# A feed-forward tail in a decode kernel: W_down loaded by 1 KB rows so that gate and up weights are read as contiguous columns

## The chip, the cores and the metric

The kernel runs on one core of one Trainium2 chip. Times are device microseconds (us) of that core, one number for each execution. A whole execution measures about 1.8 us longer than the span that its trace shows, so whole times are compared with whole times and spans with spans.

PE is the tensor engine's matmul side, PEld its weight loads (they overlap the matmuls), DVE the vector engine, ACT the scalar engine, SP the engine that issues the loads (its sequencer is SPq). PV is the product of the attention weights with V. A load has landed at the last of its semaphore updates in the trace; the views give the time from issue to landing to 0.1 us only.

## The reference, cut to what matters

One decode step for two sequences: layer norm, attention over a cache of 8192 positions and 32 heads, residual, layer norm, a gated feed-forward block, residual.

```python
B, D, F = 2, 512, 1376                    # one token each
h  = x + attention(layernorm(x), k_cache, v_cache, wq, wo)
d  = layernorm(h)
gate, up = d @ W_gate, d @ W_up           # [2, 1376]
hid = gate * (gate > 0) * up
out = h + hid @ W_down                    # [1376, 512]
```

The two caches are 268 MB; the three feed-forward matrices are 4.2 MB together.

## The kernel before

The caches stream through four buffers `slot[0..3]` of 4 MB. When the last K tile has left `slot[0]`, the three feed-forward matrices are loaded into it, with the last V tile between them, cut into four parts:

```python
for k, w in enumerate((B_W_up, B_W_gate)):
    nc.sync.dma_start(
        slot[0][:, k * DC * F:(k + 1) * DC * F],
        w.rearrange("(p c) n -> p (c n)", c=DC)).then_inc(sem_w, 16)
load_v(p + 1, vparts)                     # last V tile, four parts
nc.sync.dma_start(
    slot[0][:, 2 * DC * F:2 * DC * F + 10 * D],
    B_W_down[0:10 * 128].rearrange("(p r) n -> p (r n)", r=10)).then_inc(sem_wd, 16)
# rows 1280..1375 were loaded at the start, into wd_last [96, D]
```

Partition p holds ten successive rows of W_down, 10p to 10p + 9: one run of 10 KB. Tile f of the hidden layer therefore has to be the columns f, f + 10, f + 20, ... of W_up and W_gate, so that column 10p + f comes out on partition p:

```python
wup, wgt = ...                            # each [128, DC = 4, F = 1376] in slot[0]
def ffn_in(dst, w, f0, f1):
    for f in range(f0, f1):               # FC = 11 tiles: ten of 128 columns, one of FR = 96
        fw = 128 if f < 10 else FR
        for c in range(DC):
            i = nc.tensor.matmul(
                dst[0:fw, f * B:(f + 1) * B],
                lhsT=w[:, c, f:1280:10] if f < 10 else w[:, c, 1280:F],
                rhs=d_b[:, c * B:(c + 1) * B], start=(c == 0), stop=(c == DC - 1))
    return pe.run(i)

FH = 6
t_u = ffn_in(Sp[1], wup, 0, FC)                                    # PE S, 44 matmuls
t_g = (ffn_in(Op[1], wgt, 0, FH), ffn_in(Wp, wgt, FH, FC))         # PE O, 24; PE W, 20
# ... DVE: u_sb <- up; hd <- max(gate, 0) * u_sb, in two halves ...
pe.wait((sem_wd, 32))
# ... 44 matmuls with W_down as weights (line 515), then the last sum o_c and the output
```

The weights are the stationary operand (`lhsT`), and each matmul streams only two columns (B = 2): every matmul of this tail is a weight load of 128 x 128 with next to no arithmetic behind it.

The softmax here doesn't subtract the row's maximum and nothing guards it: scores larger than these inputs give would overflow.

## Time and profile before

| | before |
|---|---|
| whole time, median | 679.52 us (679.33 to 679.94, 4 runs) |
| span of the trace | 678.2 us |
| HBM read rate over the span | 414 GB/s |
| last wait for V is over, its PV matmuls start | 664.28 us |
| gate and up matmuls (line 473) on the chain | 2.79 + 1.39 + 1.25 = 5.43 us |
| W_down lands | 641.29 + 26.65 = 667.94 us |
| first matmul with W_down starts | 672.68 us |

From the page of the kernel before: the DMA share of 40 equal slices of the span in tenths (9 is 90% or more), what the DMA moved in GB/s, and what the chain that ended last is made of.

```profile
DMA  9999999999999999999999999999999999999991
GB/s 375 427 432 376 430 431 430 429 428 430 428 429 430 432 430 432 430 432 427 430 428 429 426 429 427 431 432 432 431 432 430 429 431 425 429 429 393 416 406 58
DMA 73%; DVE 24%; PE 1%; issue 1%; SPq 0%; DVEq 0%
```

The loads bound the kernel, in every slice but the last one. The only place where a faster matmul can count is that last slice, where no load is waited for any more. The chain of waits in order of time (start, duration, what) shows it, from the last V part on:

```profile
640.14 24.09 DMA slot<-in_A_v_cache_dram
...
664.28 1.45 PE O L334 x48
...
667.03 0.17 DVE d_b L458
667.21 0.14 issue
667.34 2.79 PE S L473 x44
670.13 1.39 PE O L473 x24
671.51 1.25 PE W L473 x20
672.77 0.05 PE S L502 x2
672.82 1.49 PE O L515 x44
```

After 664.28 us everything is a chain of PE and DVE pieces, and line 473 is more than half of it. Why it is slow stands in the groups of instructions by shape (line, engine, operation, out<-in, shapes, count; busy us, mean ns of one; idle before):

```profile
L334 PEld LDWEIGHTS O<-e,slot 128*128 128x128 bf16 x256 | 7.3, 105 | 1.7 <-DMA slot<-in_A_v_cache_dram 1.7
L473 PEld LDWEIGHTS S<-d_b,slot 128*128 128x128 bf16 x40 | 2.4, 156 | 0.4 <-issue 0.4
L515 PEld LDWEIGHTS O<-hd,slot 128*128 128x128 bf16 x40 | 1.4, 118 | 0.0
L473 PEld LDWEIGHTS S<-d_b,slot 128*96 128x96 bf16 x4 | 0.4, 194 | 0.0
```

Four weight loads, three of them of the same 128 x 128 size. Line 334 (PV) reads contiguous columns, line 515 columns 4 elements (8 bytes) apart, line 473 columns 10 elements (20 bytes) apart. Loads and matmuls overlap, so the durations are not the pace; the pace is the distance between the starts of two matmuls in the trace: 26.7, 33.3 and 58.3 ns in the same order. The tile of 96 columns, contiguous though it is, comes every 80 ns.

### The profile page before, as it was taken

How to read it: one execution, taken by the hardware profiler on the slowest of the kernel's cores; microseconds unless marked ns; L12 is line 12 of the kernel's file. 1: busy time of each engine (PE TensorE's matmuls, PEld its weight loads, DVE VectorE, ACT ScalarE, POOL GpSimd, SP SyncE). 2: the span in 40 equal slices, each digit the busy share in tenths (PEclk: the TensorE clock that was granted, in tenths of full speed). 3: DMA queues.
4: the chain of work that ended last, by engine and by line, in shares of the span. 5: the costliest groups of instructions: out<-in, count | busy, mean ns of one | idle time of the engine just before them, and what ended most of it. 6: DMA issues, size and time to landing. Idle time of an engine off the chain costs nothing.

```text
span 678.2 us, 14430 instructions
## 1 busy us (share of the span) xinstructions
PE 297.5 (44%) x6596; PEld 269.5 (40%) x6596; DVE 493.6 (73%) x428; ACT 202.3 (30%) x523; POOL 1.7 (0%) x11
## 2 busy tenths in 40 slices
PE   2552254344544424454443435444344634433356
PEld 2442244333434424343443334434334634433355
DVE  1774577778777768877777787776788867777981
ACT  0630332233333213333322333332223333222430
POOL 0000000000000000000000000000000000000000
PEclk9999999556556556556555565555565555555555
DMA  9999999999999999999999999999999999999991
GB/s 375 427 432 376 430 431 430 429 428 430 428 429 430 432 430 432 430 432 427 430 428 429 426 429 427 431 432 432 431 432 430 429 431 425 429 429 393 416 406 58
DMA packets 14785, 281.97 MB, mean 416 GB/s; under 512 B 1443, under 2 KB 5637, under 8 KB 5765
## 3 DMA queue, kind: packets, MB, share of 16 engines
q1 hardware_dynamic: 14720, 281.06, 97.4%
q8 instruction: 51, 0.84, 0.5%
q14 instruction: 10, 0.07, 0.0%
q10 hardware_dynamic: 4, 0.00, 0.0%
HBM read 281.05 MB, written 0.00 MB: 414 GB/s over the span
## 4 chain that ended last, share of the span: by engine, by line
DMA 73%; DVE 24%; PE 1%; issue 1%; SPq 0%; DVEq 0%
DMA slot<-in_A_k_cache_dram 69%; DVE prod L366 15%; DVE tb L374 5%; DMA slot<-in_A_v_cache_dram 4%; DVE prod L374 3%; DVE scores L381 1%; PE S L473 0%; PE O L515 0%; PE O L334 0%; PE O L473 0%; PE W L473 0%; SPq L353 0%; SPq L135 0%; SPq L428 0%; PE W L309 0%
## 5 line engine op out<-in xcount | busy, mean ns | idle before, releaser
L366 DVE TENSOR_TENSOR prod<-slot,q_b 128x6144 bf16<-128x6144 bf16 x64 | 214.9, 3358 | 132.3 <-DMA slot<-in_A_k_cache_dram 131.1
L334 PE MATMUL O<-e,slot 128*128 128x2 bf16 x4096 | 118.7, 165 | 239.7 <-ACT e L267 120.2
L334 PEld LDWEIGHTS O<-e,slot 128*128 128x128 bf16 x4096 | 114.5, 104 | 243.9 <-ACT e L267 122.8
L397 ACT ACTIVATE kT<-T 128x1024 bf16<-128x1024 bf16 x128 | 126.8, 1022 | 169.9 <-PE T L391 168.8
L391 PE MATMUL T<-ident,slot 128*128 128x128 bf16 x1024 | 123.4, 307 | 76.7 <-DMA slot<-in_A_k_cache_dram 75.2
L374 DVE TENSOR_TENSOR tb<-prod 128x3072 bf16<-128x3072 bf16 (+1 forms) x128 | 148.2, 1158 | 4.4
L391 PEld LDWEIGHTS T<-ident,slot 128*128 128x128 bf16 x1024 | 100.2, 141 | 79.7 <-DMA slot<-in_A_k_cache_dram 78.2
L267 ACT ACTIVATE e<-scores 64x48 bf16<-64x48 f32 x128 | 32.8, 256 | 253.6 <-DVE scores L381 252.0
L374 DVE TENSOR_TENSOR prod<-tb 128x1536 bf16<-128x1536 bf16 (+1 forms) x128 | 84.2, 658 | 4.4
L259 PE MATMUL S<-qT,kT 128*128 128x2 bf16 x1024 | 48.4, 168 | 38.6 <-ACT kT L397 37.3
L259 PEld LDWEIGHTS S<-qT,kT 128*128 128x128 bf16 x1024 | 41.0, 107 | 57.4 <-ACT kT L397 57.4
L381 DVE TENSOR_REDUCE scores<-prod 128x48 f32<-128x384 bf16 x64 | 35.4, 553 | 2.2
L267 ACT ACTIVATION_READ_ACCUMULATOR e<-scores 64x1 f32 x128 | 23.6, 185 | 0.0
L267 ACT ACTIVATE e<-S 64x32 bf16<-64x32 f32 x64 | 13.0, 203 | 15.1 <-PE S L259 14.3
L267 ACT ACTIVATION_READ_ACCUMULATOR e<-S 64x1 f32 x64 | 12.8, 201 | 0.7
L241 ACT ACTIVATE q_b<-O 128x512 bf16<-128x512 f32 x8 | 4.3, 596 | 15.5 <-PE O L236 15.5
L212 DVE CAST qT<-W 128x64 bf16<-128x64 f32 x1 | 0.2, 225 | 11.9 <-PE W L207 11.9
L309 PE MATMUL W<-O_sb,X 128*128 128x2 bf16 (+1 forms) x136 | 5.0, 172 | 7.0 <-DVE O_sb L297 7.0
L309 PEld LDWEIGHTS W<-O_sb,X 128*128 128x128 bf16 x136 | 4.8, 118 | 7.2 <-DVE O_sb L297 7.2
L207 PE MATMUL W<-xlT,X 128*128 128x2 bf16 x128 | 3.6, 165 | 8.5 <-DMA X<-in_A_wq_dram 8.5
L207 PEld LDWEIGHTS W<-xlT,X 128*128 128x128 bf16 x128 | 3.5, 104 | 8.6 <-DMA X<-in_A_wq_dram 8.6
L285 DVE TENSOR_REDUCE zr<-O 128x16 f32<-128x48 f32 (+1 forms) x4 | 0.8, 204 | 8.3 <-PE O L277 8.3
(58 smaller groups left out, 44.4 us busy)
## 6 DMA issues: line engine op xcount, KB each, us to landing
slot<-in_A_k_cache_dram SPq DMA_DIRECT2D x32, 4096.0 KB, 27.8
slot<-in_A_v_cache_dram SPq DMA_DIRECT2D x31, 4096.0 KB, 32.1
X<-in_A_wq_dram SPq DMA_DIRECT2D x1, 4096.0 KB, 12.2
X<-in_A_wo_dram SPq DMA_DIRECT2D x1, 4096.0 KB, 49.0
slot<-in_A_v_cache_dram SPq DMA_DIRECT2D x1, 1536.0 KB, 21.6
slot<-in_B_W_up_dram SPq DMA_DIRECT2D x1, 1376.0 KB, 9.8
slot<-in_B_W_gate_dram SPq DMA_DIRECT2D x1, 1376.0 KB, 16.3
slot<-in_A_v_cache_dram SPq DMA_DIRECT2D x1, 1280.0 KB, 24.1
```

Source lines behind the costliest of these rows:

```text
L207: i = nc.tensor.matmul(Wp[:, h * B:(h + 1) * B], lhsT=wq[:, c, h * Dh:(h + 1) * Dh], rhs=lT[:, c * B:(c + 1) * B], start=(c == 0), stop=(c ...
L241: t_cp[m] = act.run(nc.scalar.activation(out=q_b[:, m * 512:(m + 1) * 512], in_=Op[m % 2][:], func=ACT.Copy))
L259: i = nc.tensor.matmul(Sp[p % 2][:, 2 * jj:2 * jj + 2], lhsT=kT[n % 3][:, k * 128:(k + 1) * 128], rhs=qT[:, 2 * p:2 * p + 2], start=True, ...
L267: t = act.run(nc.scalar.activation(out=e_t[p % 2][q, j0:j0 + nj, a], in_=src(q, a), func=ACT.Exp, scale=inv_sqrt_dh, accum_out=zs[q, 2 * p ...
L285: dve.run(nc.vector.tensor_reduce(out=zr[:, 2 * p0:2 * p1], in_=zbank(k)[:, 64:64 + n * (NCH + 1)].rearrange("p (n k) -> p n k", k=NCH + 1 ...
L309: i = nc.tensor.matmul(Wp[:, c * B + b0:c * B + b1], lhsT=wo_m[:, h, c, :], rhs=Ov[:, h // 2, h % 2, b0:b1], start=first[0], stop=last, sk ...
L334: i = nc.tensor.matmul(Op[k % 2][:, col:col + 2], lhsT=v_t[:, j, :], rhs=e_t[p % 2][:, j, :], start=(nmm == 0), stop=(nmm == J - 1))
L366: t_dm = dve.run(nc.vector.tensor_tensor(out=prod[:], in0=k_t[:, c * JC:(c + 1) * JC, :], in1=qv, op=ALU.mult))
L374: dve.run(nc.vector.tensor_tensor(out=o, in0=cur[:, :, 0:half], in1=cur[:, :, half:w], op=ALU.add))
L381: t_s = dve.run(nc.vector.tensor_reduce(out=sc[:], in_=cur, axis=AX.X, op=ALU.add))
L391: i = nc.tensor.transpose(Tp[n % 3][:, k * 128:(k + 1) * 128], k_t[:, j, :], ident[:])
L397: t_ev[n] = act.run(nc.scalar.activation(out=kT[n % 3][:], in_=Tp[n % 3][:], func=ACT.Copy))
```

## The change

The intent is to read the gate and up weights in contiguous columns. Tile f becomes columns 128f to 128f + 127, so hidden unit 128r + p sits on partition p, and W_down has to follow: row 128r + p goes to partition p, place r. In HBM those rows are 128 KB apart, and the load becomes 1280 runs of 1 KB in place of 128 runs of 10 KB.

```diff
                         nc.sync.dma_start(
-                            slot[0][:, 2 * DC * F:2 * DC * F + 10 * D],
-                            B_W_down[0:10 * 128].rearrange("(p r) n -> p (r n)", r=10)).then_inc(sem_wd, 16)
+                            slot[0][:, 2 * DC * F:2 * DC * F + 10 * D].rearrange("p (r n) -> p r n", n=D),
+                            B_W_down[0:10 * 128].rearrange("(r p) n -> p r n", p=128)).then_inc(sem_wd, 16)
...
-                                dst[0:fw, f * B:(f + 1) * B], lhsT=w[:, c, f:1280:10] if f < 10 else w[:, c, 1280:F],
+                                dst[0:fw, f * B:(f + 1) * B], lhsT=w[:, c, f * 128:f * 128 + fw],
```

## The prediction

> **What bounds the kernel now.** The load of the caches: the page shows 414 GB/s over the 678.2 us span, DMA busy above 90% in 39 of 40 slices, and a chain that is 73% DMA. The change touches only the tail. In the chain in order of time the last V piece is waited for until 664.2 us; then PE and DVE run alone to the end. There the gate and up matmuls (L473) run from 667.34 to about 672.63 us, 5.3 us, all on the chain; the down matmuls (L515) follow until 674.3.
>
> **Removed.** Start to start in the trace, at a granted clock of 0.50: the 80 full-width L473 matmuls, whose weight columns step 10 elements (20 bytes), come every 58.3 ns; their weight loads last 155 ns. The 8 narrow ones (96 columns, contiguous already) come every 80 ns. Matmuls with contiguous weights of the same 128 x 128 shape come every 26.7 ns (L334, PV, at 0.50; L207 the same at 1.00), weight load 104 ns. With a step of 4 elements (L309, L515) it is 33.3 ns. So reading the weights sets the pace. The Trainium skill, page "SBUF — State Buffer", section "Specifications (TRN2)", says cachelines are 16 bytes and each crossing to a new line costs; the trace's 26.7 / 33.3 / 58.3 ns for steps of 2 / 8 / 20 bytes agree in order.
> Saving: 80 x (58.3 - 26.7) = 2.5 us, all on the critical path: DVE's copy of u (0.18 us) and the first hd product (0.17 us) keep hiding behind the remaining gate matmuls (0.64 and 0.75 us), and vh is ready by 668.0.
>
> **Added.** W_down's 1.31 MB come in 1280 rows of 1 KB instead of 128 of 10 KB. In the trace a 10 KB packet takes 385 ns (38.5 ns per KB); W_o, loaded in 1 KB rows with the same 128 KB pitch, moved at about 348 GB/s against 430, that is 47 ns per KB and engine. An engine has 80 KB of W_down, so the load takes 3.8 us rather than 3.1: 0.7 us later. Now it lands at 667.9 us (issue 641.29, 26.6 us to landing), 4.7 us before its first use at 672.7. After: estimated landing 668.7, first use about 670.15. About 1.4 us of slack is left, so the slower load stays hidden. It is queued behind V, so V's landing should not move. Its issue may block the queue longer (a K issue after W_o was held 24.6 us), which harms nothing: only the output follows.
>
> **Predicted.** 679.57 - 2.5, plus a little for the chance that W_down is waited for: 677.2 us, range 676.4 to 678.7. Faster by over 2%: 0.5%; within 2%: 99%; slower: 0.5%. The gain is about 0.35%, four times the spread of the three runs (0.6 us).
>
> **What would show it.** L473 every 27 ns (weight load 104 ns), its 88 matmuls in 2.8 us; L515 starting 2.9 us after the d_b subtraction ends and still every 33 ns; the V landing near 664.2; W_down's time to landing 27 to 28 us, and no DMA piece of W_down in the chain of waits; about 1150 more packets under 2 KB.
>
> **What would make it wrong.** W_down landing after 670.2, if its many rows are issued or moved slower than W_o's by the few late engines; then up to all of the gain goes into a wait before L515. Or its small packets on early engines slowing the V pieces that others still load. Or contiguous weights not at 26.7 ns here. A change of over 2% would need the cache stream itself to move, which nothing here touches.

## The result, and the profile after

| | before | after |
|---|---|---|
| whole time, median | 679.52 us (679.33 to 679.94, 4 runs) | 677.57 us (677.15 to 677.79, 4 runs) |
| span of the trace | 678.2 us | 675.6 us |
| last wait for V is over, its PV matmuls start | 664.28 us | 664.30 us |
| line 473 on the chain | 5.43 us | 2.92 us |
| W_down lands | 667.94 us | 641.34 + 26.93 = 668.27 us |
| first matmul with W_down starts | 672.68 us | 670.19 us |

The ratio is 0.997 (95% interval 0.9952 to 0.9987). Ratios here are the mean time of one kernel's fast runs over that of the other's of the same rounds, so not quite the ratio of the medians quoted. By the 2% rule the verdict is "same", and the gain is clear of the noise all the same.

The page of the kernel after, the same lines (slices, and the chain's shares):

```profile
DMA  9999999999999999999999999999999999999993
DMA 73%; DVE 24%; PE 1%; issue 1%; SPq 0%; DVEq 0%
```

Nothing moved in the stream of the caches. The chain of waits in order of time:

```profile
640.20 24.05 DMA slot<-in_A_v_cache_dram
...
664.30 1.46 PE O L334 x48
...
667.05 0.17 DVE d_b L458
667.23 0.14 issue
667.36 1.53 PE S L473 x44
668.89 0.64 PE O L473 x24
669.53 0.75 PE W L473 x20
670.28 0.05 PE S L502 x2
670.33 1.48 PE O L515 x44
```

The two chains run in step to 0.02 us up to line 473, and from there the new one is shorter by 5.43 - 2.92 = 2.51 us. No load stands between the gate matmuls and line 515: W_down is not waited for. The groups by shape, of the kernel after:

```profile
L473 PEld LDWEIGHTS S<-d_b,slot 128*128 128x128 bf16 x40 | 1.2, 104 | 0.4 <-issue 0.4
L515 PEld LDWEIGHTS O<-hd,slot 128*128 128x128 bf16 x40 | 1.4, 117 | 0.0
L473 PEld LDWEIGHTS S<-d_b,slot 128*96 128x96 bf16 x4 | 0.4, 186 | 0.0
```

The wide tiles of line 473 now load like those of line 334, and in the trace their matmuls start every 26.7 ns. Line 515, whose weights keep their layout, did not change. The narrow tile did not either: 80 ns from start to start, 8 times.

The clock that the throttle granted to PE differs between the two traces as a whole (0.607 and 0.551 on average), but not where it matters. Stretches of the span in the kernel before and then in the kernel after (columns: length; busy us of PE, PEld, DVE, ACT, POOL; granted clock; DMA share; GB/s):

```profile
667.30:670.30 3.00, 2.96 (x50) 2.99 (x51) 0.72 (x5) 0.00 (x0) 0.00 (x0) 0.50 0.02 5
```

```profile
667.30:670.30 3.00, 2.94 (x94) 2.97 (x95) 0.96 (x6) 0.00 (x0) 0.00 (x0) 0.50 0.04 11
```

At the same clock of 0.50, and PE busy throughout in both, the stretch that held 50 matmuls now holds 94: all 88 of line 473 and the first of the lines behind it.

### The profile page after: what moved, and what is told of

It reads as the page before. It is cut to its first block, busy times and chain, and to the rows that moved or that the text cites. A ratio compares the mean times of both kernels' runs of the same rounds, so it can differ in the third digit from the quotient of the medians.

```text
span 675.6 us, 14430 instructions
## 1 busy us (share of the span) xinstructions
PE 294.0 (44%) x6596; PEld 266.2 (39%) x6596; DVE 493.6 (73%) x428; ACT 202.0 (30%) x523; POOL 1.7 (0%) x11
## 2 busy tenths in 40 slices
DMA packets 15936, 281.97 MB, mean 417 GB/s; under 512 B 1442, under 2 KB 6916, under 8 KB 7044
## 4 chain that ended last, share of the span: by engine, by line
DMA 73%; DVE 24%; PE 1%; issue 1%; SPq 0%; DVEq 0%
DMA slot<-in_A_k_cache_dram 69%; DVE prod L366 15%; DVE tb L374 5%; DMA slot<-in_A_v_cache_dram 4%; DVE prod L374 3%; DVE scores L381 1%; PE S L473 0%; PE O L515 0%; PE O L334 0%; SPq L353 0%; SPq L135 0%; SPq L428 0%; PE W L473 0%; PE O L473 0%; PE W L309 0%
```

## The experiments

The comparison with the reference passed for every run below, those that are wrong included (two of them pair the wrong hidden units with the rows of W_down, two read arbitrary columns). So passing says nothing here about the order of rows and columns; that the changed kernel, and the one with a wider last tile below, pair them correctly is argued from the index arithmetic alone.

Theory A: the gain is the 80 wide weight loads of line 473, 58.3 to 26.7 ns each, all of it on the chain, and the load by 1 KB rows costs nothing because it hides in a slack. Rival B: the 1 KB rows give part of it back (four runs showed a mean gain of 2.06 us, the traces 2.5 us). Rival C: the load by rows itself brings part of the gain.

### The two halves apart, and more rounds

Three of the four kernels on one chip (the fourth, e4_wide_last, is further below). `e0_after` is the changed kernel. `e1_cols_only` has only the new columns:

```diff
-  lhsT=w[:, c, f:1280:10] if f < 10 else w[:, c, 1280:F],
+  lhsT=w[:, c, f * 128:f * 128 + fw],
```

`e2_load_only` is the changed kernel with the old line put back there, so only the load differs from before.

> The changed kernel again, with more rounds, because its four runs gave 2.0 us of gain (679.52 to 677.57) where the two traces' tails differ by 2.5 us (output issued 674.79 and 672.29). Theory A (the gain is 2.5 us and the rest is spread of the runs): mean gain 2.3 to 2.7 us. Theory B (something outside the tail gives 0.4 to 0.5 us back, for example V arriving later): gain 1.8 to 2.2 us, and the last V wait would end at 664.6 or later in the trace. Either way the profile should again show the last V wait ending near 664.25 and the output issued 8.0 us after it.

> Only the matmul half of the change: contiguous weight columns, W_down still loaded by 10 KB rows (the result is wrong on purpose). Theory A: the whole gain is here, the same as the full change, 2.3 to 2.7 us, with W_down landing near 667.9. Rival B (the 1 KB rows give part back): this one is faster than the full change by 0.4 to 0.5 us. Rival C (the load itself brings part of the gain): this one gains clearly less than the full change.

> Only the load half of the change: W_down by 1 KB rows, matmul columns still 10 elements apart (the result is wrong on purpose). Theory A: no change, within 0.2 us of the kernel before, W_down landing 0.3 to 0.7 us later than 667.9 with over 4 us to spare. Rival B: slower by 0.4 to 0.5 us. Rival C: faster.

The kernel before had 679.91 us (679.59 to 680.65, 9 runs). "Tail" is the distance, in the one trace of each kernel, from the start of the last 48 PV matmuls to the start of the last sum o_c; "W_down after V" is its landing counted from the same start.

| | whole time, median (5 runs each) | difference of the means | tail | W_down after V |
|---|---|---|---|---|
| before (its first trace) | 679.91 us | | 674.41 - 664.28 = 10.13 us | 3.66 us |
| e0_after | 677.30 us (676.95 to 677.51) | -2.63 us | 671.57 - 663.94 = 7.63 us | 3.98 us |
| e1_cols_only | 677.30 us (677.04 to 677.52) | -2.63 us | 671.25 - 663.63 = 7.62 us | 3.79 us |
| e2_load_only | 679.75 us (679.53 to 680.19) | -0.09 us | 674.09 - 663.95 = 10.14 us | 3.98 us |

The ratios to the kernel before are 0.9963, 0.9963 and 1.0 (intervals 0.995 to 0.9975 twice, and 0.9987 to 1.0014). These intervals reach about 0.9 us to each side, too far to rule out the 0.4 us of rival B. What rules it out is the comparison within the call: the means of e0_after and e1_cols_only agree to 0.01 us, with 0.5 to 0.6 us between the slowest and the fastest run of each, and their tails agree to 0.01 us. So the columns alone give the whole gain, and the load alone gives none and takes none: rivals B and C fall. The chain of waits has the new pace in e1_cols_only and the old one in the load-only kernel:

```profile
666.69 1.53 PE S L473 x44
668.22 0.64 PE O L473 x24
668.86 0.75 PE W L473 x20
```

```profile
667.02 2.79 PE S L473 x44
669.80 1.39 PE O L473 x24
671.19 1.25 PE W L473 x20
672.44 0.05 PE S L502 x2
672.50 1.48 PE O L515 x44
```

The expectation for e0_after of a V wait ending near 664.25 was missed by 0.3 us: it ended at 663.94; the output was issued 8.0 us after that, as expected. Over the twelve traces of these kernels it ends between 663.63 and 664.46, while the tail of a given kernel repeats to 0.02 us. So the spread from run to run lies outside the tail: ahead of it, and also behind it, where the time from the start of o_c to the end of the whole execution runs from 5.3 to 5.9 us in the same twelve traces. That is large enough for small sets of runs to give 2.06, 2.63 and (below) 2.22 us for the same change. What moves the V landing and the end was not traced.

### How much slack W_down has

A dummy load of 5 or 9 rows of 1 KB for each partition, into a buffer that nobody reads, is put between V and W_down (in the second kernel 9 in place of 5):

```diff
+        pad = sb("pad", [128, 5 * D], BF16)
...
                         load_v(p + 1, vparts)
+                        nc.sync.dma_start(
+                            pad[:], B_W_down[0:5 * 128].rearrange("(p r) n -> p (r n)", r=5)).then_inc(sem_pad, 16)
```

> The changed kernel with a dummy load of 5 KB rows (0.66 MB) between V and W_down, which puts W_down off by about 40 KB per engine x 38.5 ns = 1.5 us, to about 669.9. The changed kernel's first W_down matmul came at 670.33 and W_down landed at 668.3, so there should be 2.0 us to spare: no change of time within 0.3 us if that is the true slack. If the slack is smaller than I read it (if the wait for W_down already ends last), the time rises by up to 1.5 us.

> The same with 9 KB rows (1.18 MB): W_down put off by about 2.8 us to about 671.1, that is 0.8 us after it is wanted. If the slack is 2.0 us the time rises by 0.6 to 1.0 us over the changed kernel and W_down's load appears in the chain of waits before L515. If the matmuls did not really need to wait for it, no change.

Measured beside the kernel before at 679.95 us (679.75 to 680.11, 7 runs): with 5 KB 677.01 us (676.92 to 677.5, 4 runs), with 9 KB 678.18 us (677.9 to 678.51, 4 runs). The first keeps the whole gain (2.81 us by the means). In its trace W_down lands at 641.63 + 28.1 = 669.7 us, and its first matmul starts at 670.08, not held up; the tail is 671.81 - 664.18 = 7.63 us. The second gives part of the gain back: its tail is 672.93 - 664.46 = 8.47 us, 0.85 us longer than the 7.62 us of the changed kernel, within the expected 0.6 to 1.0. (By whole times it is 1.08 us slower than the 5 KB kernel; its V wait also ended 0.28 us later.) The start of the second's chain of waits, and one of its waits (who waited for whom: us, times, longest):

```profile
642.32 28.82 DMA slot<-in_B_W_down_dram
671.14 0.05 issue
671.19 1.64 PE O L519 x44
```

```profile
PE O L519 <- DMA slot<-in_B_W_down_dram: 0.7, 1, 0.7
```

Now the load is on the chain, and V, DVE and the gate matmuls are not: W_down lands at 671.14 us, and line 519 (line 515 of the kernel before) starts 0.05 us later. So the wait is real, and the changed kernel passes it with 670.19 - 668.27 = 1.92 us to spare. A version with much more to load in that place would pay for it.

### What the pace of a weight load depends on

The changed kernel, with another column step for each of the 20 wide tiles (a wrong result), so that one trace holds a ladder of steps:

```diff
-  lhsT=w[:, c, f * 128:f * 128 + fw],
+  lhsT=ladder(f, c, k),       # slot[0][:, c * F : c * F + step * 127 + 1 : step], step = STEPS[k][f]
```

> A measurement of the weight read by itself: the changed kernel with a different column step for every tile of L473 (wrong result on purpose): up tiles 0 to 9 with steps 1, 2, 3, 4, 5, 6, 7, 8, 9, 10 elements of 2 bytes, gate tiles 0 to 9 with steps 12, 14, 16, 20, 24, 32, 10, 8, 2, 1. Theory L (cost is per new 16-byte line): spacing rises from 26.7 ns at step 1 to about 58.3 ns at step 8, by the number of lines that 128 columns touch, and stays at 58.3 ns for every step from 8 to 32; step 4 is 33.3 ns. Rival S (cost grows with the step): step 16 and 32 come clearly slower than step 10. Rival F (a step of any size loses a fast mode): step 2 is already at 58 ns. If pairs of 8-byte units count, step 3 lies at or below step 4.

> The ladder again in another order (wrong result on purpose): up tiles 0 to 9 with steps 24, 10, 32, 16, 12, 20, 9, 7, 5, 3 elements, gate tiles 0 to 9 with steps 48, 40, 28, 24, 10, 18, 4, 6, 2, 1. In the first ladder the spacing followed the number of 16-byte lines up to step 8 (60 ns) and was 58 to 69 ns beyond it, with step 24 at 69 ns and step 10 once at 65 and once at 60 ns. If the level beyond 8 is flat and the rest is the place in the sequence, step 24 comes at 58 to 63 ns here in at least one of its two places. If step 24 has a cost of its own, both are near 69 ns. Steps 5, 7, 9, 6 should repeat 39, 54, 61 and 47 ns whatever their place.

Each ran once, in 678.64 and 679.39 us, which is of no use beyond the trace.

Each tile has four matmuls. The distance from the start of a matmul to that of the one behind it, without the first of the four, averaged over the other three (worked out from the starts in the two traces; granted clock 0.50):

```
step, elements            1     2     3     4     5     6     7     8     9    10
16-byte lines touched    16    32    48    64    80    96   112   128   128   128
first ladder, up, ns   27.7  26.7  28.3  31.7  38.7  47.3  53.7  60.7  62.0  62.7
second ladder, ns      26.7  26.7  27.7  31.7  39.0  47.3  54.7     -  59.0  62.3, 58.3

step, elements           12    14    16    18    20    24    28    32    40    48
first ladder, gate, ns 60.7  62.7  61.7     -  58.3  68.7     -  66.0     -     -
second ladder, ns      62.7     -  62.3  62.0  59.3  69.7, 68.0  61.3  67.3  61.7  66.3
```

Up to step 3 a floor of about 27 ns holds. From step 4 to 8 the pace rises in a straight line with the number of 16-byte lines that 128 columns touch: 31.7 ns for 64 lines, 47.3 for 96, 60.7 for 128, which is 0.47 to 0.50 ns a line. With 8-byte units step 4 would already be the worst, with 32-byte units step 16 would be twice step 8; neither is so. Beyond 8, where every column is on a line of its own, it stays between 58 and 70 ns. The expectation of a strictly flat 58.3 ns was too simple: step 24 came at 68 to 70 ns in all three of its places, and 32 and 48 at 66 to 67, while 20, 28 and 40 did not. (Step 10 came at 58 to 63 ns, with 59.0 in a second place of the first ladder.) For 24, in three places, that is a property of the step and not of its place in the sequence; 32 stood in two places and 48 in one only. What makes it stays open. In the second ladder steps 5, 6 and 7 repeated within 1 ns, as expected; step 9 came at 59.0 ns, where 61 was expected. Rival S (the cost grows with the step) and rival F (any step loses a fast mode) fall: step 48 costs no more than step 24, and step 2 costs nothing.

The durations of the loads vary too, as far as a view that mixes the steps can show it. The first ladder's loads of the up half, as the view of one line shows them (min, median and max of a load in ns, mixed steps and the narrow tile):

```profile
L480 PEld LDWEIGHTS S<-d_b,slot x44: 104/145/198, 666.9 to 668.8; 128*128 128x128 bf16 x40, 128*96 128x96 bf16 x4
```

The Trainium skill says in "SBUF — State Buffer", section "Specifications (TRN2)", that SBUF has 16-byte cachelines and needs at least two hits a line for full bandwidth. The ladder agrees with the line size and nearly with the threshold: step 4, two hits a line, costs 5 ns over the floor; step 5 costs 12.

### The tile of 96 columns

The narrow tile comes every 80 ns although its columns touch. The page "TensorE: Matmul & The Clock Gate" of the Trainium skill, section "Weight-path perf modes — Fast Weight Load (FWL) and DoubleRow", says the fast weight load needs the full 128 columns, and its section "LDWEIGHTS (loading the stationary operand)" puts a load at the number of columns over 1.2, in ns. An estimate from that page is 96 / 1.2 = 80 ns; the trace has 80 ns from start to start (the load itself is recorded with 186 to 194 ns). The section does not say for which mode its figure holds: for 128 columns it gives 107 ns, and the pace here is 26.7. If the missing fast mode is the reason, more columns should be cheaper. `e4_wide_last` computes columns 1248 to 1375, and the 32 that tile 9 has already meet rows of zeros:

```diff
-  wd_last = sb("wd_last", [FR, D], BF16)
+  wd_last = sb("wd_last", [128, D], BF16)
-  nc.sync.dma_start(wd_last[:], B_W_down[F - FR:])...
+  nc.sync.dma_start(wd_last[128 - FR:], B_W_down[F - FR:])...
+  pool.run(nc.gpsimd.memset(wd_last[0:128 - FR], 0.0))
...
-  fw = 128 if f < 10 else FR
+  c0 = f * 128 if f < 10 else F - 128
-  dst[0:fw, f * B:(f + 1) * B], lhsT=w[:, c, f * 128:f * 128 + fw],
+  dst[:, f * B:(f + 1) * B], lhsT=w[:, c, c0:c0 + 128],
...
-  pe.wait((sem_wd, 32))
+  pe.wait((sem_wd, 32), t_const)
-  rhs=hd[0:kp, f * B:(f + 1) * B]
+  rhs=hd[:, f * B:(f + 1) * B]
```

It ran in the call of the two halves, and again beside the changed kernel on another chip.

> The full change plus a last tile of 128 columns instead of 96 (columns 1248 to 1375; the 32 that are computed twice meet zero rows of the last W_down tile, so the result stays right). In the traces a 96-column weight load takes 194 ns and its matmuls come every 80 ns. If it is the width that costs, these 8 come every 26.7 ns and the tail is 8 x 53.3 = 0.43 us shorter than with the full change; gain over the kernel before about 2.9 us. If it is the place in memory or the position at the end of a group, the spacing stays at 80 ns and the time is that of the full change. W_down is then needed at about 669.9 and landed at 668.3, so no wait for it is expected.

> The changed kernel once more beside the next one, on whatever chip this call gets: gain over the kernel before 2.3 to 2.7 us, as the tail says (7.6 us from the last V matmuls to the output sum, against 10.1 us).

> The 128-column last tile once more, to see whether its 0.42 us in the tail shows in the whole time: 0.3 to 0.6 us faster than the changed kernel of the same call, 2.7 to 3.1 us faster than the kernel before. The tail from the last V matmuls to the output sum should again be 7.2 us.

| | before | changed kernel | 128-column last tile | tail of the last |
|---|---|---|---|---|
| first call, median | 679.91 us (9 runs) | 677.30 us (5 runs) | 676.85 us (676.57 to 677.26, 5 runs) | 671.00 - 663.80 = 7.20 us |
| second call, median | 679.56 us (9 runs) | 677.36 us (677.14 to 677.51, 5 runs) | 676.96 us (676.45 to 677.26, 5 runs) | 671.63 - 664.44 = 7.19 us |

The chain of waits of e4_wide_last (line 474 is line 473 of the others):

```profile
666.87 1.31 PE S L474 x44
668.18 0.64 PE O L474 x24
668.82 0.53 PE W L474 x20
```

So the width costs, as the page says; the mode itself is not in the trace. All 88 matmuls now start 26.7 ns apart, and the tail is 7.62 - 7.20 = 0.42 us shorter than the changed kernel's, against 8 x 53.3 ns = 0.43 expected. By the means of whole times it is 0.36 us (677.29 to 676.93) and 0.47 us (677.35 to 676.88) faster than the changed kernel, with ranges that overlap a little; against the kernel before 2.99 and 2.70 us (ratios 0.9957 and 0.9959, intervals 0.9945 to 0.997 and 0.9945 to 0.9973). It beats both kernels. Its first matmul with W_down came at 669.27 us, not at the expected 669.9, and W_down landed at 668.24, so this kernel has 1.0 us to spare (1.5 in e9_wide_last) in place of 1.9. The second call's changed kernel gained 2.22 us by the means, just short of the 2.3 expected, with a tail of 671.68 - 664.06 = 7.62 us.

## Why the prediction was right, and where its sizes were off

- The bound and the place. It said that the stream of the caches would not move and that only the tail would. The V wait ended at 664.28 and 664.30 us, and the chains agree to 0.02 us up to line 473. Right.
- The removed cost. It said 80 x (58.3 - 26.7) = 2.5 us, all on the chain. The chain lost 2.51 us on line 473, the columns alone gave the same tail as the full change (7.62 us), and DVE's pieces stayed hidden. Right.
- The reason for it. Cachelines of 16 bytes were taken from the skill with three points behind them. The ladders have since put twenty steps behind it; it holds up to step 8, with steps of 24, 32 and 48 dearer than it explains.
- The added cost. It put the load 0.7 us later, from "47 ns per KB and engine" as W_o's rows moved. This term was mis-sized. In the trace's packet records, which do not name the engine, the last run of back-to-back packets, taken as one engine's 80 KB, lasted 3.07 us before and 3.39 after, 42 ns a KB. W_down landed 3.98 to 4.00 us after the V wait in seven of the eight traces that have short rows and no dummy load (4.43 in the eighth, e4_wide_last), against 3.66 and 3.79 with long rows (before, e1_cols_only): 0.2 to 0.3 us later, but for the one. W_o's rate was taken while all 16 engines moved short rows; here, at the end, fewer were at work (the DMA share was 0.37 between 664.2 and 667.3 us in the kernel after, and 1.10 while W_o moved). That fewer engines at work is the reason was not tested.
- The slack. It said 1.4 us; the trace has 1.9 us, because the load came earlier than reckoned (668.27 against 668.7 us), and the two dummy loads confirm it: they put the landing, counted from the V matmuls, at 5.53 and 6.68 us in place of 3.98, and the delay of 1.5 us cost nothing, that of 2.7 us 0.85.
- "About 1150 more packets under 2 KB" was a slip: that is the rise of all packets (14785 to 15936), for 128 long ones went. Under 2 KB there are 6916 - 5637 = 1279 more.
- "W_down's time to landing 27 to 28 us": it was 26.9, for the same reason as the slack.
- The time. 677.2 us was predicted, 677.57 measured, within the range. The first four runs gained 2.06 us by the means; two further calls with five runs of the changed kernel each gained 2.63 and 2.22. The tail's 2.5 us lies among them, and the difference is within the spread of what comes ahead of the tail and behind it.

## What to carry to other kernels

Where a matmul streams few columns (two here), its pace can be the read of its weights: look at the distance between starts, and choose the layout so that successive weight columns share 16-byte lines (steps of up to 3 two-byte elements cost at most 2 ns here, step 4 a fifth more) and that a tile has all 128 columns, even if some are computed twice (26.7 ns for 128 here, 80 for 96). Pay for that layout in a load that hides, and check the slack of that load by delaying it. In a kernel bound by loads such a change is worth only what stands behind the last load, so read its worth from the chain's tail and not from the busy shares; a few tenths of a per cent need the trace, for the spread of whole times (0.6 us in four runs of the kernel before) was a quarter of the gain.

## What the Trainium skill lacked or had wrong

- "TensorE: Matmul & The Clock Gate", "LDWEIGHTS (loading the stationary operand)": the pace of weight loads by column step is not there. Measured for 128 x 128 bf16 tiles with two streamed columns: 27 ns up to step 3, then 31.7, 39, 47, 54 and 60.5 ns for steps 4 to 8, 58 to 63 for most steps up to 40, and 66 to 70 for steps 24, 32 and 48.
- "SBUF — State Buffer", "Door 1: The DMA port swizzle": it says one can stride 8 bf16 elements for free (beside its own demand for two hits a line, which a step of 8 cannot meet). For weight loads that is not so: step 8 comes every 60 ns against 27.
- "DMA: Bandwidth & Descriptors", "Specifications": it gives 512 B as the least transfer for line rate. Rows of 1 KB at a pitch of 128 KB did not reach it here: W_o moved at 348 GB/s, against about 430 with rows of 32 KB (from the kernel before, the stretch below, with the columns as above). Whether the row or the pitch costs was not tested.

```profile
56.00:58.00 2.00, 0.00 (x0) 0.00 (x0) 1.90 (x4) 0.00 (x0) 0.00 (x0) 1.00 1.10 348
```
